# Strassen's seven half-size products for the second FFN product of six token groups

## The chip, the cores and the metric

The kernel runs on one core of a Trainium2 chip. The metric is the device time of one execution in microseconds (us). Times of one kernel agree to about 0.3%, so a difference of 0.5% can be read, but not one of 0.1%. Engines are named as in the profile: PE is TensorE, PEld its weight loads, DVE VectorE, ACT ScalarE, SP the issuer of the transfers.

Executions come in two kinds that differ by some 1.5 us: mean granted TensorE clock 1.000 or 0.999, or 0.997 to 0.998. The kernel before has both kinds (793.4 and 795.0). Where a microsecond matters, executions of the first kind are compared, and the text says so.

## The reference, cut to what matters

```python
def _attn_ref(x, filt_r, filt_i):            # x: 8 x 3008 x 256
    X = np.fft.rfft(x, axis=1)
    Y = X * (filt_r + 1j * filt_i)[None]
    return np.fft.irfft(Y, n=x.shape[1], axis=1)

def _moe_ref(x, w_in, w_out):                # x: 24064 x 256, w_in: 256 x 2048, w_out: 2048 x 256
    h = np.maximum(x @ w_in, 0.0)
    return h * h @ w_out
```

An FFT filter along the sequence feeds a feed-forward network with a squared ReLU. The change concerns only the last product, `h*h @ w_out`.

## The kernel before

The FFN works on 47 groups of 512 tokens, 8 slots a group. In slot k of group g, TensorE makes two blocks of h (four 512-column matmuls), ScalarE applies ReLU, VectorE squares. In the same slot TensorE makes an eighth of the second product of group g-1 (eight 256-column matmuls). FFT work of later batches is spread over the slots; the last of it, inverse transforms called `unit_y`, ends in slot 332. Each engine runs its instructions in program order.

```python
def ffn_g1(g, s):                      # first product and ReLU
    ...
    nc.tensor.matmul(ps[:, i, o:o + n], sWin[:, dt, jt * 128:(jt + 1) * 128],
                     yts[b][:, dt, r:r + n], start=(dt == 0), stop=(dt == 1))
    ...
    nc.scalar.activation(out=h2[:, 2 * s:2 * s + 2, :], in_=ps, func=AF.Relu)

def ffn_sq(g, s):
    v = h2s[g][:, 2 * s:2 * s + 2, :]
    nc.vector.tensor_mul(out=v, in0=v, in1=v)

def ffn_g2(g, s):                      # second product: weights are blocks of h, w_out moves
    t, half = divmod(s, 2)
    ...
    for jt in range(8 * half, 8 * half + 8):
        nc.tensor.matmul(pso[g][:, t % 2, :], h2s[g][:, jt, t * 128:(t + 1) * 128],
                         sWout[:, jt, :], start=(jt == 0), stop=(jt == NJT - 1))

for s in range((NG + 1) * SLOTS):      # the slot loop; NG = 47, SLOTS = 8
    g, k = divmod(s, SLOTS)
    ffn_g1(g, k); run(work, s, 0); ffn_g2(g - 1, k); run(work, s, 1)
    ffn_out(g - 1, k); ffn_sq(g, k)    # guards for the first and last group cut
```

## Time and profile before

| what | value | read from |
|---|---|---|
| time | 793.5 us | median of the runs |
| TensorE busy | 98% of the span | busy shares |
| one slot without FFT work | 1.74 us | start of one L562 row to the next |
| one group without FFT work | 13.89 us | eight slots |
| second product, matmul pitch | 0.109 us | row starts, not durations |

In the busy table each row is a stretch (start, end, length), then PE, PEld, DVE, ACT and POOL busy, the granted clock and the transfers. This is one group of before, slots 336 to 343, with no FFT work:

```profile
711.79:725.68 13.89, 13.89 (x98) 9.39 (x96) 5.53 (x8) 9.14 (x11) 0.00 (x0) 1.00 0.13 39
```

TensorE fills the stretch and VectorE works 40% of it. That spare 60% is what the change wants to spend.

### The profile page before, as it was taken

The numbers are of one execution on the slowest core, as the hardware profiler recorded it, in microseconds if no ns is written. First come the engines' busy times: TensorE is split into PE (matmuls) and PEld (weight loads), VectorE is DVE, ScalarE is ACT, GpSimd is POOL, SyncE is SP. The second block draws the span as 40 slices with busy tenths as digits, with TensorE's granted clock in tenths as the row PEclk, the third lists the DMA queues.
The fourth block names the chain that finished last, engine by engine and source line by source line (L and its number), as shares of the span: only waits on it lengthen the run. The fifth ranks groups of instructions, "written<-read, shape, count | busy, mean of one in ns | idle before, by whom it ended". The sixth has DMA issues, their size and how long they took to land.

```text
span 791.9 us, 14822 instructions
## 1 busy us (share of the span) xinstructions
PE 778.9 (98%) x6102; PEld 552.5 (70%) x6102; DVE 550.3 (69%) x897; ACT 557.4 (70%) x711; POOL 23.6 (3%) x36
## 2 busy tenths in 40 slices
PE   8989999999999999999999999999999999999998
PEld 5746667667676777867777676776767677676666
DVE  6866994579755897559965699556995579553342
ACT  3976776777777777767776777676777777776664
POOL 3800000000000000000000000000000000000000
PEclk9999999999999999999999999999999999999999
DMA  9994554346814557154562555424563332611111
GB/s 363 368 260 153 146 157 111 93 135 167 205 42 112 167 155 180 48 173 135 132 167 65 163 147 155 112 80 148 159 180 86 97 133 66 147 40 41 41 41 54
DMA packets 88571, 107.32 MB, mean 136 GB/s; under 512 B 6336, under 2 KB 79040, under 8 KB 84288
## 3 DMA queue, kind: packets, MB, share of 16 engines
q1 hardware_dynamic: 88296, 106.19, 46.5%
q8 instruction: 48, 0.79, 0.4%
q10 hardware_dynamic: 144, 0.18, 0.1%
q14 instruction: 19, 0.16, 0.1%
q0 software_dynamic: 64, 0.00, 0.0%
HBM read 58.12 MB, written 48.23 MB: 134 GB/s over the span
## 4 chain that ended last, share of the span: by engine, by line
PE 89%; DVE 6%; DMA 3%; ACT 1%; SPq 0%; issue 0%; DVEq 0%; ACTq 0%
PE psO L579 40%; PE psH L562 38%; PE psA L361 3%; PE psY L532 2%; PE psB L445 2%; DMA f<-in_filt_i_dram 2%; PE psP L496 2%; DVE prod L453 2%; DVE h L570 1%; DMA wout<-in_moe_w_out_dram 1%; PE psf L287 1%; PE psf L290 1%; DVE yf L467 0%; ACT sF L298 0%; DVE yf L461 0%; ACT h L566 0%
## 5 line engine op out<-in xcount | busy, mean ns | idle before, releaser
L566 ACT ACTIVATE h<-psH 128x1024 f16<-128x1024 f32 x376 | 384.9, 1024 | 189.3 <-PE psH L562 186.7
L579 PE MATMUL psO<-sWout,h 128*128 128x256 f16 x3008 | 388.9, 272 | 0.6 <-DVE h L570 0.6
L562 PE MATMUL psH<-yt,sWin 128*128 128x512 f16 (+7 forms) x1728 | 386.9, 351 | 1.6 <-DVE yt L541 0.7
L579 PEld LDWEIGHTS <-h 128*128 128x128 f16 x3008 | 290.6, 98 | 79.1 <-DVE h L570 0.9
L570 DVE TENSOR_TENSOR h<-h 128x1024 f16<-128x1024 f16 x376 | 252.6, 685 | 104.7 <-ACT h L566 104.5
L562 PEld LDWEIGHTS <-sWin 128*128 128x128 f16 x1728 | 159.5, 98 | 101.7 <-issue 3.3
L453 DVE TENSOR_TENSOR prod<-psB,sF 128x1024 f16<-128x1024 f32 x84 | 102.3, 1218 | 2.8 <-PE psB L445 2.8
L541 DVE CAST yt<-psY 128x376 f16<-128x376 f32 x62 | 34.0, 549 | 59.4 <-PE psY L532 59.4
L367 DVE CAST u<-psA 96x512 f16<-96x512 f32 x50 | 34.3, 687 | 47.3 <-PE psA L361 45.1
L498 ACT CAST ze<-psP 128x512 f16<-128x512 f32 x84 | 49.1, 585 | 17.2 <-PE psP L496 14.7
L590 ACT COPY ost<-psO 128x512 f32<-128x512 f32 (+1 forms) x96 | 55.8, 581 | 6.8 <-PE psO L579 5.3
L532 PE MATMUL psY<-sC,zt 112*128 112x94 f16 x512 | 42.4, 205 | 1.4 <-DMA zt<-dZ 1.4
L532 PEld LDWEIGHTS <-zt 112*128 112x128 f16 x512 | 35.1, 98 | 11.6 <-issue 1.6
L467 DVE TENSOR_TENSOR yf<-prod,yf 128x512 f16<-128x512 f16 x84 | 35.7, 425 | 2.9
L361 PE MATMUL psA<-x,sC 94*96 94x512 f16 x96 | 36.6, 382 | 0.0
L445 PE MATMUL psB<-ut,sSB 128*128 128x256 f16 x192 | 36.5, 273 | 0.0
L496 PE MATMUL psP<-yf,sSP 128*128 128x256 f16 x168 | 32.1, 272 | 0.5 <-DVE prod L453 0.3
L539 ACT CAST yt<-psY 128x376 f16<-128x376 f32 x66 | 30.9, 468 | 2.0 <-issue 1.7
L445 PEld LDWEIGHTS <-sSB 128*128 128x128 f16 x192 | 18.5, 98 | 19.5
L340 DVE CAST x<-x 94x2048 f16<-94x2048 f32 x24 | 29.2, 1216 | 0.0
L365 ACT CAST u<-psA 96x512 f16<-96x512 f32 x50 | 28.6, 572 | 0.0
L460 DVE COPY yf<-prod 64x512 f16<-64x512 f16 x84 | 24.3, 289 | 2.9
(65 smaller groups left out, 253.2 us busy)
## 6 DMA issues: line engine op xcount, KB each, us to landing
x<-in_x_dram SPq DMA_DIRECT2D x20, 768.0 KB
zt<-dZ SPq DMA_DIRECT2D x64, 192.0 KB
dU<-u SPq DMA_DIRECT2D x28, 384.0 KB
dZ<-ze SPq DMA_DIRECT2D x28, 384.0 KB
out_dram<-ost SPq DMA_DIRECT2D x66, 128.0 KB
out_dram<-ost SPq DMA_DIRECT2D x31, 256.0 KB
ut<-dU SPq DMA_DIRECT2D x7, 1024.0 KB
xw<-in_x_dram SPq DMA_DIRECT2D x6, 1024.0 KB
```

The costliest lines, as they stand in the source:

```text
L361: nc.tensor.matmul(ps[0:96, :], sSA, x16s[(b, c)][:, m, :], start=True, stop=True)
L445: nc.tensor.matmul(ps[:, i * D:(i + 1) * D], sSB[:, 2 * p + i, :], uts[b][:, 2 * p + i, :], start=True, stop=True)
L453: nc.vector.tensor_mul(out=prod, in0=ps.rearrange("p (a d) -> p a d", d=D).unsqueeze(1).to_broadcast([128, 2, 2, D]), in1=sF[:, :, 2 * p:2 ...
L467: nc.vector.tensor_add(out=yf, in0=prod[:, 0], in1=yf)
L496: nc.tensor.matmul(ps[:, i * D:(i + 1) * D], sSP[:, 2 * p + i, :], yf[:, i, :], start=True, stop=True)
L498: nc.scalar.copy(out=zes[(b, c)][:, 2 * i6:2 * i6 + 2, :], in_=ps.rearrange("p (a d) -> p a d", d=D))
L532: nc.tensor.matmul(ps[:, 94 * jj:94 * jj + 94], zt[:, 4 * (g % 2) + jj, dt * 128:(dt + 1) * 128], sSY, start=True, stop=True)
L562: nc.tensor.matmul(ps[:, i, o:o + n], sWin[:, dt, jt * 128:(jt + 1) * 128], yts[b][:, dt, r:r + n], start=(dt == 0), stop=(dt == 1))
L566: nc.scalar.activation(out=h2[:, 2 * s:2 * s + 2, :], in_=ps, func=AF.Relu)
L570: nc.vector.tensor_mul(out=v, in0=v, in1=v)
L579: nc.tensor.matmul(pso[g][:, t % 2, :], h2s[g][:, jt, t * 128:(t + 1) * 128], sWout[:, jt, :], start=(jt == 0), stop=(jt == NJT - 1))
L590: nc.scalar.copy(out=ost[:, h0:h0 + step, :], in_=pso[g][:, h0:h0 + step, :])
```

## The change

Strassen's scheme, in the form with shared sums, multiplies 2x2 blocks with seven products of half size instead of eight. Here h of a group (512 tokens by 2,048) and w_out are cut into quarters. TensorE's columns for the second product fall by an eighth, from 64 matmuls of 256 columns to 112 of 128. In exchange VectorE makes four sums of quarters of h a group, and adds of partial results from PSUM. The sums of w_out are made once (`make_t`). Products start one slot later than the second product did. Groups 40 to 45 use it, the stretch with almost no FFT work.

```diff
+    def make_t():
+        t = p_x32.tile([128, 4, 8, 128], F16, tag="x32", name="sT")
+        ...                                    # four sums of quarters of w_out
+    def sums(g, k):
+        a11, a12, a21, a22 = quads(g)
+        if k == 0:
+            t = p_x16.tile([128, 8, D], F16, tag="x16", name=f"s3_{g}")
+            nc.vector.tensor_sub(out=t, in0=a11, in1=a21)        # for product 7
+            nc.vector.tensor_add(out=a21, in0=a21, in1=a22)      # for product 5
+            sg[g] = {1: a11, 2: a12, 4: a22, 5: a21, 7: t}
+        elif k == 1:
+            ...
+            nc.vector.tensor_sub(out=t, in0=a21, in1=a11)        # for product 6
+        elif k == 3:
+            ...
+            nc.vector.tensor_sub(out=t, in0=a12, in1=sg[g][6])   # for product 3
+    PARTS = (((1, 0, 16),), ((5, 0, 8), (6, 0, 6)), ((6, 6, 16), (5, 8, 12)),
+             ((5, 12, 16), (7, 0, 10)), ((7, 10, 16), (2, 0, 8)), ((2, 8, 16), (4, 0, 6)),
+             ((4, 6, 16), (3, 0, 4)), ((3, 4, 16),))
+    def products(g, k):
+        for p, m0, m1 in PARTS[k]:
+            o = f["x"][:, 0] if p in (1, 6, 7, 4) else f["y"][:, 0 if p == 2 else 1]
+            ...                                # matmuls m0 to m1 of product p into o
+            # after 1, 6, 7, 4: ScalarE copies o; after 2 and 3: VectorE adds from PSUM
...
+    SEVEN = range(40, NG - 1)
...
+        if s == SEVEN[0] * SLOTS:
+            make_t()
+        if (s - 1) // SLOTS - 1 in SEVEN:
+            products((s - 1) // SLOTS - 1, (s - 1) % SLOTS)
-        if g > 0:
+        if g > 0 and g - 1 not in SEVEN:
             ffn_g2(g - 1, k)
...
+        if g - 1 in SEVEN:
+            sums(g - 1, k)
         if g < NG:
             ffn_sq(g, k)
```

## The prediction

> **What bounds the kernel now.** I read the page first, then the groups of instructions by form, the waits and busy table of the last part of the run, then the timeline of one slot. A slot is one step of the FFN loop: four first-product matmuls (L562), then eight second-product matmuls (L579). The page's busy shares:
>
> ```profile
> PE 778.9 (98%) x6102; PEld 552.5 (70%) x6102; DVE 550.3 (69%) x897; ACT 557.4 (70%) x711; POOL 23.6 (3%) x36
> PEclk9999999999999999999999999999999999999999
> ```
>
> TensorE is busy 98% of the span at the full granted clock, so to a first approximation the time is the sum of its work plus its stalls. Groups 40 to 45 have their second products in slots 328 to 376, after the FFT work has ended except for the last inverse transforms (psY). The busy table of that pure-FFN stretch:
>
> ```profile
> 707.00:783.00 76.00, 76.00 (x541) 52.14 (x540) 30.64 (x45) 49.26 (x54) 0.00 (x0) 1.00 0.11 36
> ```
>
> After window and length come PE, PEld, DVE, ACT and POOL busy. TensorE has no gap; VectorE works 30.64 of 76 us. The waits there name VectorE waiting for ScalarE and ScalarE for TensorE, and never TensorE:
>
> ```profile
> DVE h L570 <- ACT h L566: 44.7, 43, 1.1
> ACT h L566 <- PE psH L562: 25.9, 43, 0.7
> ```
>
> One slot in time (start, duration):
>
> ```profile
> 743.05 1.03 PE L562 MATMUL psH<-yt,sWin 128*128 128x512 f16 x4
> 743.91 1.04 PE L579 MATMUL psO<-sWout,h 128*128 128x256 f16 x8
> 744.11 1.02 ACT L566 ACTIVATE h<-psH 128x1024 f16<-128x1024 f32 x1 [0.71 <-PE psH L562]
> ...
> 745.17 0.69 DVE L570 TENSOR_TENSOR h<-h 128x1024 f16<-128x1024 f16 x1 [1.05 <-ACT h L566]
> ```
>
> Matmul rows overlap, so pitch counts, not duration: L562 takes 743.91-743.05 = 0.87 us a slot, and L579 0.87 too (the next L562 starts at 744.79), 0.109 each. Squaring of a slot's h ends 2.81 us after the slot's first matmul (745.17+0.69-743.05).
>
> **Pitch of small matmuls.** The change makes 128-column matmuls, each with a new stationary block. The nearest forms are the 96-column products of the prologue and the 128-column turns (by-form groups: L422, mean 219 ns, against 272 ns for 256 columns):
>
> ```profile
> 10.27 0.21 PE L403 MATMUL psA<-sC,xw 128*128 128x96 f16 x1
> ...
> 13.23 0.21 PE L403 MATMUL psA<-sC,xw 128*128 128x96 f16 x1
> ```
>
> ```profile
> 20.79 0.61 PE L422 MATMUL psT<-sC,uT 128*128 128x128 f16 x8
> ```
>
> In the first fence 66 pitches, each with its own weight load, take 2.96 us: 0.045 us. In the second eight take (0.61-0.22)/7 = 0.056 us. Loads of 128x128 blocks thus keep up even at 96 columns.
>
> **What the Trainium skill says.** "TensorE: Matmul & The Clock Gate", "Back-to-back issue gap", gives N/2.4 + 2.5 ns for a lone stream (55.8 at N=128, 109 at 256), but 81 ns for sustained load-and-multiply pairs at N=128. This trace agrees with the first (56 and 109 ns), not the second. "VectorE: DVE Perf Modes", "The perf-mode tier table", has tensor_tensor on 2,048 16-bit elements at 1,224 ns. The trace has 425 ns for 512 (L467) and 685 for 1,024 (L570), 0.51 ns an element, so 685+520 = 1.21 us: agreement. "What auto-detection actually checks" on that page asks 16-bit tensors and step 1 for two elements a cycle. The quarters keep inner runs of 256 at step 1, but no strided two-input 16-bit operation in this trace confirms it. "PSUM — Partial Sum Buffer", "PSUM bank collisions raise a hardware error", wants accesses of two engines to a bank kept apart by semaphores; so a product that accumulates onto a bank that ScalarE or VectorE reads must wait for that read. The trace of before has no such mid-sum read.
>
> **The change part by part.**
> *TensorE removed and added.* Per group 64 x 0.1088 = 6.96 us goes; 7 x 16 = 112 matmuls at 0.056 = 6.27 us come. Gain 0.69 us a group, 4.15 us for six.
>
> *ScalarE.* Two 128x512 copies a group (0.58 each) become four of 128x256 (0.37 in the by-form groups): +0.3 us on an engine with over a third idle. Each copy has a first product's time or more (over 1 us) before the same bank is written again. Not on the path.
>
> *VectorE.* Per group four sums of 2,048 elements (1.21 each) and three adds of 256 from PSUM. L453's 1,218 ns for 1,024 fp32 elements and L541's 549 for 376 give 1.04 ns an element plus 0.15, so 0.42 each. That is 6.1 us beside 5.5 of squaring, in some 13.2 us of slots: it fits on average. What matters is when the sums come.
>
> *When, in the steady groups.* Clock zero is the first matmul of slot 8(G+1). TensorE's order is fixed: L562 0.87, last product of the group before (12 x 0.056 = 0.67), L562 0.87, product 1 (0.90), L562 0.87, the eight matmuls of product 5 (0.45), then product 6. Without stalls product 5 is reached at 4.17 and product 6 at 4.62. VectorE, also in program order (each slot's squaring comes last on it): squaring of G's last slot is done at 2.81-1.65 = 1.16; then the add of the former product 3, which waits for that product to leave the array (1.54+0.16), 1.7 to 2.1. Two independent operations in a row overlap by some 0.08 us ("x2" rows of L570 last 1.29, not 1.37). So the first sum ends at 3.3, the second (a21+a22, product 5's operand) at 4.4, the squaring of the new slot runs 4.36 to 5.05, and the third sum (product 6's operand), emitted a slot later behind that squaring, ends at 6.18. With 0.15 us from release through weight load to matmul (a psP wait on VectorE at 93.8 us shows 0.04, a load lasts 0.10), product 5 starts at 4.6 and product 6 at 6.33. TensorE has lost 6.33-4.62 = 1.71 us. Later VectorE catches up: the fourth sum ends near 9, over 2 us before product 3. So each of five groups nets +1.71-0.69 = +1.02.
>
> *The first group, 40.* Slot 328 has no second product, and VectorE has make_t's four 128x1024 operations (about 0.65 each with overlap, 2.6) ahead of the cast of a psY and the sums. From zero at that slot (696.10 in the trace), squaring ends at 1.35, make_t at 3.87, the cast at 4.35, the two sums at 5.5 and 6.6, a squaring at 7.2, another psY cast 7.67, the third sum 8.8; product 6 at 8.95. TensorE's work before it is 3 x 0.87 + 0.90 + 0.45 + five psY units at 0.17 = 4.8. Stall 4.1 (parts: psY waiting for psF, then products 5 and 6), net +3.4.
>
> *Sum.* Stalls 4.1 + 5 x 1.71 = 12.7, gain 4.15: +8.5 us on 793.5, so 802. The end of the kernel (group 46, from slot 376) is as before.
>
> **The rivals.**
> 1. *The sums hide and the arithmetic gain stands.* For it: VectorE's 40% load. Against: the fixed order, which leaves it 3 us between the last squaring and product 6 for 3.6 us of sums, 0.6 of squaring and a wait of about 0.5. It would make 789 to 790, still within 2%.
> 2. *Sums at one element a cycle.* The strided form could fall out of the two-element rate: each would take 2.28 us. The third sum then ends 3.2 us later in five groups, and 3.2 plus some 2 of make_t later in the first: about 823. The step-1 inner runs speak against it.
> 3. *Weight loads bind 128-column matmuls* at 81 ns: 9.07 us a group, 2.1 more than before; 36 of those matmuls stand before product 6 and eat 0.9 of its stall, so 2.9 a group, some 812. The 66 pitches at 0.045 speak against it.
> 4. *Waits of p6, p7, p4 on the PSUM copies add up.* The ScalarE copy sits behind a 1.02 us activation, but the next product on that bank is over 1 us of TensorE work away: perhaps 0.1 to 0.3 a group in the worst case, up to +2 us in all.
>
> **Range and chances.** My centre is 802; the stall per group could be 1.2 to 2.3 (release latency, overlap), which is 799 to 806. Rival 1 pulls to 790, rivals 2 and 3 push beyond 809.4, the 2% line. 8 in 10: 793 to 811. Faster by over 2% needs 16 us where the arithmetic holds 4: 1 in 100. Slower by over 2%: 10 in 100. Within: 89.
>
> **What would show it.** Right: new TensorE waits on VectorE sums before product 5 and more before product 6, 1.5 to 2 us a group and about 4 in the first; 128-column matmuls in runs at 0.056 pitch; sums at 1.2 us; no psH or psX wait. Wrong: no gaps after 696 us (rival 1), sums over 2 us (rival 2), product rows at 0.08 pitch without waits (rival 3), TensorE waiting on ScalarE copies (rival 4).

## The result, and the profile after

The median went from 793.54 to 800.05 us; the ratio is 1.0085, with a 95% interval of 1.007 to 1.01. (Ratios here are of the fast runs of both kernels in the same rounds; they are not quite the ratios of the medians.) By the 2% rule this is "same", but it is clearly a small loss. The busy shares of the whole run, to be held against those in the prediction:

```profile
PE 777.0 (97%) x6390; PEld 552.3 (69%) x6390; DVE 585.5 (73%) x943; ACT 558.3 (70%) x723; POOL 23.7 (3%) x36
```

TensorE has less busy time than before (777.0 against 778.9 us) in a longer run. So it waits more. The busy table of one changed group, slots 336 to 343 again:

```profile
712.02:726.94 14.92, 13.51 (x148) 9.31 (x146) 10.98 (x15) 9.29 (x13) 0.00 (x0) 1.00 0.11 36
```

The group lasts 14.92 us instead of 13.89, and TensorE is idle for 1.41 of it. VectorE works 10.98 us, 74%: well filled, but not overloaded. The waits from 690 us on, first TensorE's weight loads, then its matmuls (total, times, longest):

```profile
PEld L665 <- DVE s L643: 8.2, 6, 1.7
PE psX L665 <- DVE s L643: 7.2, 6, 1.6
PEld L665 <- DVE h L639: 3.9, 5, 0.8
PE psY L665 <- DVE h L639: 1.5, 5, 0.3
```

There were no TensorE waits at all in the corresponding stretch of before. L643 is the third sum (product 6's operand) and L639 the second (product 5's). The timeline of VectorE and of the products in that group shows the order:

```profile
713.75 0.42 DVE L687 TENSOR_TENSOR top<-psY,u 128x256 f32<-128x256 f32 x1 [0.57 <-PE psY L665]
714.10 1.22 DVE L638 TENSOR_TENSOR s<-h 128x2048 f16<-128x2048 f16 x1
715.35 1.22 DVE L639 TENSOR_TENSOR h<-h 128x2048 f16<-128x2048 f16 x1
716.49 0.68 DVE L570 TENSOR_TENSOR h<-h 128x1024 f16<-128x1024 f16 x1
...
716.63 0.62 PE L665 MATMUL psY<-sT,h 128*128 128x128 f16 x8 [0.29 <-DVE h L639]
717.09 1.22 DVE L643 TENSOR_TENSOR s<-h 128x2048 f16<-128x2048 f16 x1
...
718.37 0.51 PE L665 MATMUL psX<-sT,s 128*128 128x128 f16 x6 [1.12 <-DVE s L643]
```

The first sum made (L638) is for product 7, which TensorE needs last of the three; it stands ahead of the two that TensorE needs at once. The squaring of the new slot (L570), wanted only a group later, stands ahead of the third. The part of the chain of waits over this group leaves TensorE for VectorE just there:

```profile
713.05 0.69 PE psY L665 x12
...
713.75 0.42 DVE top L687
714.18 1.14 DVE s L638
...
715.35 1.22 DVE h L639
716.57 0.60 DVE h L570
717.17 1.15 DVE s L643
...
718.37 0.51 PE psX L665 x6
```

Idle times in the waits understate the loss: a matmul row ends some 0.16 us after the next could have started (0.22 us long at a pitch of 0.056). In what follows the length of a steady group, from L562 row to L562 row eight slots on, is the measure: 13.89 before, 14.92 after. It repeats within 0.01 us in all four changed groups that can be read so.

### The profile page after: what moved, and what is told of

It reads as the page before. It is cut to its first block, busy times and chain, and to the rows that moved or that the text cites. A ratio compares the mean times of both kernels' runs of the same rounds, so it can differ in the third digit from the quotient of the medians.

```text
span 798.0 us, 15477 instructions
## 1 busy us (share of the span) xinstructions
PE 777.0 (97%) x6390; PEld 552.3 (69%) x6390; DVE 585.5 (73%) x943; ACT 558.3 (70%) x723; POOL 23.7 (3%) x36
## 4 chain that ended last, share of the span: by engine, by line
PE 88%; DVE 10%; ACT 1%; DMA 1%; issue 0%; ACTq 0%; DVEq 0%; SPq 0%
PE psH L562 37%; PE psO L579 34%; PE psA L361 3%; PE psY L532 2%; PE psB L445 2%; PE psX L665 2%; PE psP L496 2%; DVE h L570 2%; PE psY L665 2%; DVE prod L453 2%; PE warm L268 1%; DVE h L639 1%; DVE s L643 1%; DVE s L638 1%; PE psf L287 1%; PE psf L290 1%
## 5 line engine op out<-in xcount | busy, mean ns | idle before, releaser
L562 PE MATMUL psH<-yt,sWin 128*128 128x512 f16 (+7 forms) x1728 | 386.9, 351 | 1.7 <-DVE yt L541 0.7
L579 PE MATMUL psO<-sWout,h 128*128 128x256 f16 x2624 | 339.2, 272 | 0.6 <-DVE h L570 0.6
L570 DVE TENSOR_TENSOR h<-h 128x1024 f16<-128x1024 f16 x376 | 252.0, 684 | 74.0 <-ACT h L566 71.8
L579 PEld LDWEIGHTS <-h 128*128 128x128 f16 x2624 | 253.3, 98 | 65.9 <-DVE h L570 0.9
L562 PEld LDWEIGHTS <-sWin 128*128 128x128 f16 x1728 | 157.7, 98 | 100.7 <-issue 3.3
L453 DVE TENSOR_TENSOR prod<-psB,sF 128x1024 f16<-128x1024 f32 x84 | 102.3, 1218 | 2.7 <-PE psB L445 2.7
L541 DVE CAST yt<-psY 128x376 f16<-128x376 f32 x62 | 34.1, 549 | 55.5 <-PE psY L532 55.4
L590 ACT COPY ost<-psO 128x512 f32<-128x512 f32 (+1 forms) x84 | 48.7, 580 | 7.7 <-PE psO L579 4.0
L467 DVE TENSOR_TENSOR yf<-prod,yf 128x512 f16<-128x512 f16 x84 | 35.7, 425 | 2.9
L665 PEld LDWEIGHTS <-h 128*128 128x128 f16 x384 | 23.9, 98 | 9.0 <-DVE h L639 3.9
```

The costliest lines, as they stand in the source:

```text
L453: nc.vector.tensor_mul(out=prod, in0=ps.rearrange("p (a d) -> p a d", d=D).unsqueeze(1).to_broadcast([128, 2, 2, D]), in1=sF[:, :, 2 * p:2 ...
L590: nc.scalar.copy(out=ost[:, h0:h0 + step, :], in_=pso[g][:, h0:h0 + step, :])
L665: nc.tensor.matmul(o[:, t, :], f[p][:, q, 128 * t:128 * t + 128], sg["w"][p][:, q, :], start=(m == 0 and p in (1, 5)), stop=(q == 7), skip ...
```

## The experiments

Eleven kernels ran. "Steady group" is that length for groups whose slots hold no FFT work; times are medians of all executions.

| run | steady group, us | time, us | ratio to before | result correct |
|---|---|---|---|---|
| the change | 14.92 | 800.05 | 1.0085 | yes |
| no sums | 13.16 | 789.54 | 0.9953 | no |
| third sum earlier | 14.44 | 796.79 | 1.0045 | yes |
| needed sums first | 13.18 | 790.11 | 0.9960 | yes |
| product 2 second | 13.38 | 791.51 | 0.9977 | no |
| the same, mended | 13.38 | 791.39 | 0.9964 | yes |
| sums only | 13.89 | 794.79 | 1.0012 | yes |
| `make_t` at slot 328 | 14.91 | 805.85 | 1.0147 | yes |
| three groups | 14.92 (changed group) | 796.58 | 1.0036 | yes |
| extra operation | 17.07 (four of five) | 810.93 | 1.0212 | yes |
| add behind sums | 14.38 | 798.01 | 1.0047 | yes |
| needed first, from 39 | 13.18 | 790.25 | 0.9945 | yes |

The theory: TensorE gains about 0.7 us a group from fewer columns and loses about 1.7 waiting for two sums whose place in VectorE's order makes them late. Rivals: the small matmuls gain nothing; VectorE's load as such is the bound; PSUM copies hold TensorE.

### No sums: what the matmuls alone are worth

```diff
-            nc.vector.tensor_sub(out=t, in0=a11, in1=a21)
-            nc.vector.tensor_add(out=a21, in0=a21, in1=a22)
-            sg[g] = {1: a11, 2: a12, 4: a22, 5: a21, 7: t}
+            sg[g] = {1: a11, 2: a12, 4: a22, 5: a21, 7: u, 6: u, 3: u}   # u: a constant tile
```
(The sums in slots 1 and 3 are removed too.)

> No sums of h on VectorE: products 3, 5, 6 and 7 read raw or constant operands (the result is wrong on purpose), the same 112 matmuls a group, the same copies and adds from PSUM. Theory (TensorE gains 0.69 us a group and all the loss is waiting for sums): no TensorE wait from group 40 on, 793.5 - 4.15 = 789.4 us, between 789.0 and 790.0. Rival (128-column matmuls with a fresh weight load each, or the waits for PSUM copies, give the gain back): 793 us or more.

Measured: 789.54 us, and no TensorE wait from 695 us on. A steady group lasts 13.16 us, 0.73 less than before, so the saving that the scheme promises is real: the blocks of product rows in one group (from 711.63 to 724.79 us) take 6.25 us together, so 128-column matmuls with a fresh 128x128 block each run at 6.25/112 = 0.0558 us. The same sum in a group of before (711.79 to 725.68 us) is 6.99 us, 0.1092 a matmul. The three executions at clock 1.000 have 789.4 to 789.5, the theory's figure.

### Sums only: what the sums alone cost

The second product of before is kept for all groups; the four sums of groups 40 to 45 and `make_t` still run, into tiles that nobody reads.

> The second product of before in all groups, with the sums of h (four of 2,048 elements a group, and make_t) still done on VectorE for groups 40 to 45 and read by nobody. Theory (the sums cost nothing by themselves, only TensorE's wait for them does): 793.5 us, within 0.3. Rival (VectorE's extra load slows squaring or memory access of TensorE): 796 us or more.

Measured: 793.51, 793.97, 795.61 and 795.67. The first two ran at clock 0.999 and agree with before (793.3 to 794.3 in the rounds of that kernel); the other two at 0.998. The median of 794.79 is outside the expected band because half of four executions are of the lower clock. The profile shows no TensorE wait after 695 us, and the ratio's interval (0.9997 to 1.0027) includes 1. The times make this no sharper than about 0.3%, but the lengths of the groups do: a steady group (711.54 to 725.43 us) lasts 13.89 us, exactly as before, with VectorE busy 9.81 us of it instead of 5.53. Only group 40, whose slots hold inverse transforms too, lasts 15.91 instead of 15.69. So the sums by themselves are hidden.

### Third sum earlier: one place in the order

```diff
             nc.vector.tensor_add(out=a21, in0=a21, in1=a22)
+            t = p_x16.tile([128, 8, D], F16, tag="x16", name=f"s2_{g}")
+            nc.vector.tensor_sub(out=t, in0=a21, in1=a11)        # moved here from slot 1
```

> Only the place of the third sum (product 6's operand) changes: directly behind the second sum, ahead of the squaring of the new slot, which costs 0.61 us of pitch on VectorE. Theory (TensorE's wait before product 6 ends with that sum): each of six groups gets 0.6 us back, 800.05 - 3.6 = 796.4 us, wait before product 6 some 0.6 shorter. Rival (VectorE's total work is what counts): unchanged, 800 us, since the same operations run.

Measured: 796.79 us, a steady group of 14.44, so 0.48 saved a group instead of 0.6. The wait before product 6 in this run:

```profile
PE psX L664 <- DVE s L642: 3.8, 6, 0.6
```

The 0.12 missing is overlap. In the change the third sum starts 717.09-715.35 = 1.74 us after the second; directly behind it, and depending on it, it can start only when that one is done, 1.26 later (714.32 and 715.58 in this run). That is 0.48 earlier, which is what the group gained. (Group 40 gained more, 16.08 to 15.15 us: in its slots a cast of a psY tile had stood before the third sum as well.) The same operations run in another order and the time falls: total load is not the bound.

### Extra operation before the third sum: the dose the other way

```diff
         elif k == 1:
+            t = p_x16.tile([128, 8, D], F16, tag="x16", name=f"sx_{g}")
+            nc.vector.tensor_sub(out=t[:, 0:4, :], in0=a12[:, 0:4, :], in1=a11[:, 0:4, :])
             t = p_x16.tile([128, 8, D], F16, tag="x16", name=f"s2_{g}")
```

> One more VectorE operation of 128x1024 elements a group, read by nobody, directly before the third sum (0.61 us of pitch). Theory (every 0.61 us ahead of the third sum is lost on TensorE): 800.05 + 6 x 0.61 = 803.7 us. Rival (VectorE has idle time to absorb it): 800 us.

Measured: 810.93 us (807.2 to 813.2 in four executions), more than twice the expected rise, at mean clocks of 0.987 to 0.996. In the profiled execution group 40, which kept the full clock, went from 16.08 to 16.68 us: +0.60, as expected. Four of the five steady groups went to 17.07: +2.15. The last, group 45, lost only the 0.60 (its first seven slots take 13.88 us instead of 13.28). The timeline of TensorE in group 40 (first row) and in group 41, and the busy table around the latter (the column after POOL is the granted clock):

```profile
703.23 0.51 PE L667 MATMUL psX<-sT,s 128*128 128x128 f16 x6 [2.17 <-DVE s L645]
...
717.32 0.62 PE L667 MATMUL psY<-sT,h 128*128 128x128 f16 x8 [0.29 <-DVE h L639]
719.66 0.82 PE L667 MATMUL psX<-sT,s 128*128 128x128 f16 x6 [1.72 <-DVE s L645]
720.27 1.91 PE L562 MATMUL psH<-yt,sWin 128*128 128x512 f16 x4
```

```profile
716.00:718.00 2.00, 1.65 (x15) 0.74 (x12) 1.97 (x3) 1.56 (x3) 0.00 (x0) 1.00 0.29 91
718.00:720.00 2.00, 0.34 (x4) 0.35 (x5) 2.00 (x3) 0.09 (x1) 0.00 (x0) 0.87 0.00 0
720.00:722.00 2.00, 2.00 (x10) 0.90 (x8) 1.94 (x3) 0.00 (x0) 0.00 (x0) 0.50 0.00 0
722.00:724.00 2.00, 2.00 (x19) 1.60 (x18) 0.69 (x1) 1.33 (x2) 0.00 (x0) 0.78 0.00 0
```

Four 512-column matmuls take 1.91 us instead of 1.03: the granted clock is 0.50. From the means, it fell at about 719.5 and came back at 722.9, some 3.4 us. That costs half of 3.4, 1.7 us less what lies in the wait, and with the 0.6 explains the 2.15. So the expectation held for the wait and missed a second cost: with a wait that is only 0.6 us longer, the clock fell in four groups. The length of the wait alone does not decide it: group 40 kept the clock through a longer one (2.17), and group 45 kept it with the same two (0.29, and 1.72 before its product 6 at 787.94). What the traces show of the limit stands under "The clock" below.

### `make_t` where the prediction had placed it

```diff
-        if s == SEVEN[0] * SLOTS:
+        if s == (SEVEN[0] + 1) * SLOTS:
             make_t()
```

> make_t moved to slot 328, where the prediction took it to be (the change has it at slot 320). Theory: its four operations, 2.6 us, stand before the cast and the sums of group 40, whose third sum ends some 2.5 us later: 802.3 to 802.7 us, 2.3 to 2.6 slower than the change. Rival (VectorE catches up before product 6): 800 us.

Measured: 805.85 us, 5.8 above the change; expected were 2.3 to 2.6. In the profiled execution (806.61 us) group 40 goes from 16.08 to 21.30 us, which is 5.2 of its loss; another 1.2 us lies before slot 328, as this execution is of the second kind. The later groups are unchanged at 14.9. Its timeline has the two waits of the theory, longer than in the steady groups, and the clock falls again:

```profile
703.95 0.62 PE L665 MATMUL psY<-sT,h 128*128 128x128 f16 x8 [1.61 <-DVE h L639]
706.14 0.82 PE L665 MATMUL psX<-sT,s 128*128 128x128 f16 x6 [1.57 <-DVE s L643]
```

```profile
704.00:706.00 2.00, 0.57 (x8) 0.39 (x8) 2.00 (x3) 0.00 (x0) 0.00 (x0) 0.82 0.00 0
706.00:708.00 2.00, 1.86 (x16) 1.41 (x17) 1.37 (x4) 0.00 (x0) 0.00 (x0) 0.50 0.00 0
708.00:710.00 2.00, 2.00 (x18) 1.55 (x17) 0.46 (x1) 0.98 (x2) 0.00 (x0) 0.50 0.00 0
710.00:712.00 2.00, 2.00 (x19) 1.55 (x17) 0.86 (x2) 0.78 (x3) 0.00 (x0) 0.50 0.00 0
```

Against the 14.28 us of this group in the kernel without sums, it loses 7.0. The three waits (0.26 on a psY tile, 1.61, 1.57, each with the 0.16 of the modelled end) make 3.9; the prediction's figure for exactly this arrangement was 4.1. The other 3 us go with the clock at half for nearly 7 us. So with `make_t` at slot 328 the predicted wait would have come true, and the clock would have been missed.

### Three groups: a cost per group or of the switch?

```diff
-    SEVEN = range(40, NG - 1)
+    SEVEN = range(43, NG - 1)
```

> Seven products in groups 43 to 45 only. Theory (each later group costs 1.03, the first one, with less TensorE work before product 6 but no former product 3 to wait for, about 0.7): 793.5 + 0.7 + 2 x 1.03 = 796.3 us. Rival (a fixed cost of the switch, not one per group): 799 to 800 us.

Measured: 796.58 us, ratio 1.0036. Three groups cost 2.9 us and six cost 6.5: per group, not per switch.

### Needed sums first: the remedy on VectorE

```diff
         if k == 0:
+            t1 = p_x16.tile([128, 8, D], F16, tag="x16", name=f"s1_{g}")
+            nc.vector.tensor_add(out=t1, in0=a21, in1=a22)       # product 5; no longer in place
+            t = p_x16.tile([128, 8, D], F16, tag="x16", name=f"s2_{g}")
+            nc.vector.tensor_sub(out=t, in0=t1, in1=a11)         # product 6
+            sg[g] = {1: a11, 2: a12, 4: a22, 5: t1, 6: t}
+        elif k == 1:
             t = p_x16.tile([128, 8, D], F16, tag="x16", name=f"s3_{g}")
             nc.vector.tensor_sub(out=t, in0=a11, in1=a21)        # product 7, a slot later
+            sg[g][7] = t
```

> Sums in the order in which TensorE needs them: a21+a22 into a tile of its own, then the third sum, both in the first slot, then a11-a21 a slot later. Theory: the operands of products 5 and 6 are ready 1.2 and 1.8 us earlier, so the waits fall to under 0.15 us a group; 789.4 plus at most 0.9: 789.5 to 790.3 us, faster than both kernels. Rival (VectorE's load is the bound): above 796 us, as the same number of operations runs.

Measured: 790.11 us, ratio 0.9960 (0.9946 to 0.9973), correct. It beats both kernels. Of the waits in the changed groups none is left; the only one after 695 us is 0.2 us for a psY tile in group 40. One steady group:

```profile
710.51:723.69 13.18, 13.18 (x148) 9.39 (x146) 10.80 (x15) 9.28 (x13) 0.00 (x0) 1.00 0.12 41
```

Group 40 lasts 14.79 us, 0.51 more than without sums: two of its inverse transforms start 0.32 and 0.20 us late, each just after a cast of a psY tile, which here stands behind a sum and a squaring in VectorE's order. This is nearly all that the kernel takes more than the one without sums (790.11 - 789.54 = 0.57).

In the steady group VectorE has the same 15 operations as in the change and is a larger share of the group busy (82%, against 74%), while TensorE has no gap. This is the plainest evidence against "VectorE is too full". The tile of its own costs nothing: the pool has four buffers, and the change used three a group.

### Product 2 second: the remedy on TensorE

VectorE's order stays as in the change. TensorE makes product 2, which needs no sum, before product 5.

```diff
-    PARTS = (((1, 0, 16),), ((5, 0, 8), (6, 0, 6)), ...
+    PARTS = (((1, 0, 16),), ((2, 0, 14),), ((2, 14, 16), (5, 0, 8), (6, 0, 4)),
+             ((6, 4, 16), (5, 8, 10)), ((5, 10, 12), (7, 0, 12)), ((7, 12, 16), (5, 12, 16)),
+             ((4, 0, 16),), ((3, 0, 16),))
```
(The first matmul of product 2 now clears its bank, and the adds that followed product 2 follow product 5.)

> VectorE's order untouched; only TensorE's order of products changes: 1, 2, 5, 6, 7, 4, 3. Product 2 needs no sum, so 0.90 us of its matmuls and one more L562 block (0.87) stand before product 6. Theory: by 6.4 to 6.6 us after the slot's start product 6 finds its operand (ready at 6.3 to 6.5): waits under 0.2 us a group, 789.5 to 791 us. Rival (load on VectorE): 798 us or more.

Measured: 791.51 us, no waits for sums, but a wrong result: the add of the top left quarter still named product 5's columns. Mended, it was run again:

> The earlier kernel with product 2 second, mended: its top-left add read product 5's columns instead of product 2's, so the result was wrong. Same instructions otherwise. Theory: correct now, and the same time, 791.0 to 792.0 us. Rival (the wrong operand had hidden a wait): over 793 us.

Measured: 791.39 us, correct. A steady group lasts 13.38 us, 0.22 above the kernel without sums, though the list of waits names none in it. The timeline of the mended kernel shows where:

```profile
723.47 0.39 PE L665 MATMUL psY<-sT,h 128*128 128x128 f16 x4
723.69 1.03 PE L562 MATMUL psH<-yt,sWin 128*128 128x512 f16 x4
724.36 0.37 ACT L677 COPY pu<-psX 128x256 f32<-128x256 f32 x1
...
724.78 1.05 PE L665 MATMUL psX<-sT,h 128*128 128x128 f16 x16
```

L562 starts at 723.69 and takes 0.87, so product 4 could start at 724.56. It starts at 724.78, just after the copy of the same PSUM bank ends (724.73). This is the prediction's fourth rival, present here and absent in the change, whose product order puts other matmuls between products 7 and 4.

### Add behind sums, and one group more

In the first kernel the first two sums are put ahead of the slot's products in program order, so that VectorE does not wait for the former group's product 3.

> The first two sums are put ahead of the products of their slot in program order, so that VectorE does not wait for the former product 3 to leave the array before it starts them (waits of 0.56 in the changed kernel's trace, plus the add's 0.42, less overlap: about 0.9). Nothing else moves. Theory: in five groups the chain starts 0.8 to 0.95 earlier, the wait before product 5 goes (0.45), that before product 6 falls to some 0.8: 800.05 - 5 x 0.9 = 795.5 us. Rival (the add is behind the chain's limit anyway, squaring or ScalarE sets the start): 799 us or more.

Measured: 798.01 us; at clock 1.000 it is 797.1, and a steady group lasts 14.38, so 0.54 saved a group, not 0.9. The wait before product 5 is gone as expected, but the add, 0.33 us of pitch, now stands between the second and third sum: it is moved, not removed. The expectation had counted its removal.

In the second, the needed sums come first and group 39 uses the scheme too:

> Sums in the order of need, for groups 39 to 45, make_t in slot 318. Theory: with no wait each further group gains 0.69: 790.1 - 0.7 = 789.4 us, where VectorE, which also casts psY in slots 320 to 328, still has the operands in time. Rival (VectorE is full enough there that the waits return): 790.5 us or more.

Measured: 790.25 us. In executions at clock 0.999 or more it has 789.7 to 790.5, against 789.9 to 790.4 for groups 40 to 45: no further gain. (Its ratio of 0.9945 is low because six of before's eleven executions in those rounds were of the lower clock; the ratios of the mended kernel and of add behind sums, which shared those rounds, are low for the same reason.) The saved 0.7 is given back to one wait:

```profile
PE psX L666 <- DVE s L640: 0.6, 1, 0.6
```

It stands in group 39, before product 6 at 687.07 us. That is the rival: with other work on VectorE, the third sum is late again.

## Why the prediction was right

**TensorE's gain.** The prediction had 0.69 us a group from pitches of 0.1088 and 0.056. The kernel without sums shows 0.73 (pitches of 0.1092 and 0.0558), so 4.4 us for six. The step held, and the slower of the skill's two figures for small matmuls (81 ns) did not apply. (Half of the 66 matmuls in the prediction's first fence are L405, with 120 rows; the kernel without sums shows it for full blocks.)

**VectorE's durations.** The four sums take 1.22 us each (1,217 to 1,225 ns) and the adds 0.42, as predicted from L467, L570, L453 and L541. The second rival, one element a cycle for strided quarters, is refuted.

**The steady groups.** Product 5 was put at 4.6 us after the group's first matmul and product 6 at 6.33. They start at 716.63-712.02 = 4.61 and 718.37-712.02 = 6.35. The stall was put at 1.71; 14.92-13.16 = 1.76 was measured. Net +1.02 was predicted and 14.92-13.89 = +1.03 measured; it agrees better than its two parts because their errors, 0.05 and 0.04, cancel. The experiments show the cause, not only the size: earlier sums shorten it, an extra operation lengthens it, and either remedy of order removes it.

**The first group.** Here a step failed: "Slot 328 has no second product, and VectorE has make_t's four 128x1024 operations ... ahead of the cast of a psY and the sums." The code calls `make_t` when s is 40 x 8 = 320, a group earlier. The timeline of the changed kernel has it there:

```profile
681.80 0.68 DVE L623 TENSOR_TENSOR sT<-sWout 128x1024 f16<-128x1024 f16 x1
```

Between 681.8 and 684.4 us it delays nothing on TensorE. The stall of the first group was 16.08-14.28 = 1.80 us, not 4.1. This reading error of 2.3 us is nearly the whole distance between 802 and 800.05.

**The sum.** Stalls of 1.80 + 5 x 1.76 = 10.6, less 6 x 0.73 = 4.4, make +6.2 us; the profiled spans differ by 798.0-791.9 = 6.1. The time was within the range, in the direction and of the size foretold.

**The rivals.** The first (sums hidden, 789 to 790) did not happen, but it is what the kernel gives once the sums come in the order of need: 790.1. The third (weight loads bind) is refuted by the kernel without sums. The fourth is absent in the change and costs 0.22 us a group in another product order.

**The clock.** The prediction had no term for it, and the change needed none: its clock stayed at 1.00 with waits of 0.29 and 1.12. The clock records of the traces show how near it was. In the kernels with the extra operation and with `make_t` at slot 328, each stretch at half clock lasts 3.413 us or twice that, and the stretches between them in the changed groups are whole multiples of it too (13.653 us is four times, 34.133 ten times). Laid over TensorE's timeline, this grid gives the idle time in each window of 3.413 us (by the modelled ends of the rows). The windows just before a fall have 1.82 to 1.84 us (extra operation) and 2.33 us (`make_t`); those of the change have at most 1.57; and the wait of 2.17 in group 40 of the extra-operation kernel is split over two, 1.36 and 0.81. So these runs fit a rule that goes by the idle time within one window; the length of a single wait does not sort them.

**What stays open.** The limit itself. It lies between 1.57 and about 1.8 us in a window, but 1.82 stands on both sides: group 45 of the extra-operation kernel has it and kept the clock. No run varied it alone.

## What to carry to other kernels

An engine with spare time on average still stalls the bound engine if it makes things in another order than they are needed: write down when each operand is needed and put the producer's instructions in that order, with work for later groups behind. Measure the two halves of such a trade apart (the saving without its price, the price without its saving) before giving it up; here the saving was real, and reordering three instructions turned 0.85% slower into 0.4% faster. And find the actual place of every added instruction in program order before sizing it: one misread slot number was the prediction's largest error.

## What the Trainium skill lacked or had wrong

- "TensorE: Matmul & The Clock Gate", "Back-to-back issue gap": it gives 81 ns a matmul for sustained load-and-multiply pairs at 128 columns. Here they ran at 55.8 ns with a fresh weight block each (product rows of the kernel without sums), which is what the page's formula gives for an isolated gap, without a budget for loads.
- The same page, "Why this matters for your kernels": it advises against idle gaps over about 3 us, as one window of idle lowers the clock. Here the clock halved after windows of 3.413 us with 1.82 to 1.84 us idle, in gaps of 0.29 and 1.5 us with 0.6 us of matmuls between them (group +2.15 us for 0.6 us more waiting), so shorter gaps that fall in one window can do it. The page tells of frequent short idles that do this, under "A second HAM failure mode: psum-queue depth-cycling", but gives no length. The 3.4 us for which the clock stayed low agree with the window length that it gives under "What's actually happening".
